# Attention in a fused kernel: the neighbour-key probabilities of two heads transposed as one 128x128 block, and one softmax multiplication in place of two

## The chip, the cores and the metric

The kernel runs on one core of one Trainium2 chip. The metric is the device time of one execution in microseconds (us). Lower is better.

## The reference

Sliding-window attention over 4 sequences of 576 tokens, 8 heads of 64 features, then a product of two projections with two more matrices behind it, then a feed-forward with SiLU. All outputs are float32; the weights come as float64.

```python
scores = np.matmul(q, k.transpose(0, 1, 3, 2)) / np.sqrt(64)
mask = (rel >= 0) & (rel < 64)              # rel = position of query - position of key
attn = softmax(where(mask, scores, -1e9))   # sum + 1e-9 in the denominator
x = (attn @ v) as [2304 tokens, 512]
x = ((x @ w1) * (x @ w2)) @ w3 @ w_out      # 512 -> 1024 -> 1024 -> 512
h = x @ w_in                                # 512 -> 2048
out = (h * sigmoid(h)) @ w_out2             # 2048 -> 512
```

## The kernel before

Activations lie transposed, features on partitions. A float32 operand of a product is split into two parts, hi and lo, of type float32r, and three products of parts are summed in PSUM.

The attention is cut into 72 groups: 18 units of 128 tokens times 4 pairs of heads. A token sees itself and the 63 tokens before it, so a unit needs its own 128 keys and the 64 before them: 192 columns of scores for each head. Those 64 earlier keys matter to the unit's first 64 tokens alone. A group passes through these steps, each with its line:

- `scores` (L242, L247): two products of 192 columns, one for each head, and from group 17 on a third product of 384 columns (L247) for the low part. Groups 0 to 16 are "plain": they multiply in float32 itself, with 64 rows of the array and without L247. VectorE then adds the mask and finds the maximum (L253).
- `exps` (L264): ScalarE's exponential, in place in the tile `sm`, with the row sums in `rs`.
- `normalise` (L272 to L278): VectorE makes the reciprocal of the sums and multiplies. It does so in two instructions: the first 64 tokens' columns of the earlier keys, both heads, go to a tile of their own, `sp` (64 partitions x 128), and the columns of the own keys stay in `sm` (128 partitions x 256).
- `transposes` (L286, L287): TensorE makes three transposes into the PSUM tile `t`: two of 128x128 from `sm`, one for each head, and one of `sp`, which has 64 partitions.
- `split_t` (L293 for plain groups; L297 to L302 for the others): ScalarE and VectorE copy `t` to SBUF as hi and lo parts `pt`. Only columns 0 to 319 of `t` are read.
- `values` (L312, L313 for plain groups; L319, L320 for the others): the product with v, into `o`; L323 to L327 add its four parts into `xr`.

The order is written out by hand. `half(h)` issues half a step of this pipeline: an even half issues the transposes of group g-1, the scores of group g, the copies of `t` and the exponentials; an odd half issues normalise of group g, values of group g-1 and what prepares later groups (L219, L223, L226, L79, L82). Each engine works through its instructions in the order in which they are issued.

The halves lie between other work. In `phase_w` (up to some 115.8 us of the profile) 28 halves go between the products of w3 with w_out (L452) and the conversion of weights from float64 (L106 to L134). In `phase_a`, called for each of six blocks of 384 tokens, one half goes ahead of each of 24 units, and a unit is 12 matmuls of 384 columns (L480, then L500). The attention's halves end with the fifth block; the sixth block has none, and the feed-forward (L602, L621) follows.

The masks come by three transfers from DRAM (L418, L424, L432), in one queue with the chunks of weights (L99). The host packs q, k and v so that each group's keys are one run of 384 columns.

Of the kernel before, what the change touches and what calls it, by code (L numbers as in the profile page):

```python
# [42 lines left out]
def tile_window_attention_ffn(ctx, tc, qkv, mask, ident, w1, w2, w3t, w_out, w_in, w_out2, out):  # L43
    """Sliding window attention, then p = (x w1)(x w2), x2 = p (w3 w_out), out = silu(x2 w_in) w_out2.

    Activations are kept transposed (features on partitions). Every float32 operand of a product
    is split exactly into hi + lo, two float32r parts, and hi*hi + hi*lo + lo*hi are summed in PSUM
    (the attention's second product takes all four; w3 w_out and the first groups of the attention
    are products in float32 itself).
    """  # L50
    nc = tc.nc
# [9 lines left out]

    mask_sb = att.tile([128, 3, 192], F32, name="mask_sb", tag="mask", bufs=1)
    id_sb = att.tile([128, 128], F32, name="id_sb", tag="ident", bufs=1)
# [4 lines left out]
    def slot(name, tag, dims, dtype=F32, pool=None, bufs=1):  # L68
        """A tile [128, *dims] in a slot of the tag's size (1024 words for a chunk of weights)."""
        t = (pool or main).tile([128, SLOTS.get(tag, 1024)], dtype, name=name, tag=tag, bufs=bufs)  # L70
        n = int(np.prod(dims))
        letters = "abcd"[: len(dims)]
        sizes = {x: d for x, d in zip(letters[1:], dims[1:])}
        return t[:, :n].rearrange(f"p ({' '.join(letters)}) -> p {' '.join(letters)}", **sizes)

    def split(hi, lo, src, eng_hi, eng_lo):
        """src (float32) = hi + lo, both float32r."""
        if eng_hi == "act":
            nc.scalar.copy(out=hi, in_=src)  # L79
        else:  # L80
            (nc.vector if eng_hi == "dve" else nc.gpsimd).tensor_copy(hi, src)
        (nc.vector if eng_lo == "dve" else nc.gpsimd).tensor_tensor(  # L82
            out=lo, in0=src, in1=f32(hi), op=ALU.subtract
        )

    PASSES = ((0, 0), (0, 1), (1, 0))

# [1 line left out]
    class Chunk:  # L89
        """A chunk of weights on its way: its words are in a slot of their own, and its parts take  # L90
        that slot over (`place`), or the float32 goes to `out`."""

# [16 lines left out]
        def stage1(self):  # L109
            """Round to the nearest float32: the high word less 896 exponents, three bits further left, its sign,  # L110
            and the low word's top three bits, rounded. In parts."""
            b = self.b

            def fraction():
                nc.vector.tensor_scalar(out=b, in0=b, scalar1=3, scalar2=None, op0=ALU.logical_shift_left)  # L115

            def sign():
                nc.vector.scalar_tensor_tensor(  # L118
                    out=b, in0=self.high, scalar=-0x80000000, in1=b, op0=ALU.bitwise_and, op1=ALU.bitwise_or
                )  # L120
                x = b if self.out is None else self.out.bitcast(I32)
                nc.gpsimd.tensor_tensor(out=x, in0=b, in1=self.r, op=ALU.add)  # L122

            return fraction, sign
# [25 lines left out]
    def fill(n=1):  # L150
        """Parts of stages that go between other instructions of VectorE that wait for one another."""
        for _ in range(min(n, len(parts))):
            parts.pop(0)()

    def steps_to(n, lo=(nc.vector,), keep=0):
        """Chunk t has its stages in steps t, t + 1, t + 3 and t + 4."""
        while done["step"] < min(n, len(line)):
# [18 lines left out]

# [1 line left out]
    NG = NU * NPAIR  # L178
    LAST_HALF = 2 * NG + 2
    qk_raw, v_raw, qk_st, v_st, s_st, p_st = {}, {}, {}, {}, {}, {}  # L180
    pt = {}
    sm = [att.tile([128, 2, 192], F32, name=f"sm{i}", tag=f"sm{i}", bufs=1) for i in range(2)]
    sp = [att.tile([64, 2, 64], F32, name=f"sp{i}", tag=f"sp{i}", bufs=1) for i in range(2)]
    k_lo = [att.tile([128, 384], F32R, name=f"klo{i}", tag=f"klo{i}", bufs=1) for i in range(2)]
# [5 lines left out]
    def plain(g):  # L190
        """The first groups multiply in float32 itself: more of TensorE's time, which the start has, and
        less of the other engines'."""
        return g < PLAIN
# [42 lines left out]
    def scores(g):  # L236
# [3 lines left out]
        for h in range(2):  # L240
            # The start also marks head 1's part as unwritten.
            nc.tensor.matmul(  # L242
# [8 lines left out]
        for h in range(2):  # L251
            # -(scores), and the least of them: minus the maximum.
            nc.vector.tensor_tensor_reduce(  # L253
                out=sm[g % 2][:, h, :], in0=s_ps[:, h, :], in1=mask_sb[:, mask_kind(place(g)[0]), :],
                op0=ALU.add, op1=ALU.min, scale=-(D ** -0.5), scalar=3.0e38, accum_out=nm[:, h : h + 1],
# [12 lines left out]
    def normalise(g):  # L268
        _, rs = s_st.pop(g)
        x, before = sm[g % 2], sp[g % 2]  # L270
        fill()
# [3 lines left out]
        fill()  # L275
        for dst, src in ((before, x[0:64, :, 0:64]), (x[:, :, 64:192], x[:, :, 64:192])):
            by = rs[0 : dst.shape[0]].unsqueeze(2).to_broadcast(list(dst.shape))
            nc.vector.tensor_tensor(out=dst, in0=src, in1=by, op=ALU.mult)  # L278

    def transposes(g):  # L280
        """The scores of the unit's own keys, by head; then those of the 64 keys before (which only the
        unit's first 64 tokens see) with head 0 on partitions 0-63 and head 1 on the others."""
        x = sm[g % 2]
        t_ps = psa.tile([128, 320], F32, name=f"t{g}", tag="t")
        for h in range(2):
            nc.tensor.transpose(t_ps[:, h * 128 : h * 128 + 128], x[:, h, 64:192], id_sb)  # L286
        nc.tensor.transpose(t_ps[:, 256:320], sp[g % 2].rearrange("p h n -> p (h n)"), id_sb[0:64, 0:64])  # L287
        return t_ps

    def split_t(g, t_ps):  # L290
        if plain(g):
            p_st[g] = p_w[g % 2]
            nc.scalar.copy(out=p_st[g], in_=t_ps)  # L293
            return
# [34 lines left out]
    def half(h):  # L329
        """Half a step of the attention's pipeline: group g is in its four stages in halves  # L330
        2g .. 2g + 3."""
        g, odd = divmod(h, 2)
# [8 lines left out]
        else:  # L341
# [7 lines left out]
            if g < NG:  # L349
                prep_v(g)  # L350
            # A slot is free again when its last group has been read.
            for x in range(g + 2, g + 5):
# [20 lines left out]

# [1 line left out]
    W_HALVES = 28  # L375
# [84 lines left out]

# [1 line left out]
    def phase_a(blk, hooks):  # L462
# [55 lines left out]
    with tc.manual_schedule():  # L518
# [7 lines left out]

# [1 line left out]
        end = ctx.enter_context(tc.tile_pool(name="end", bufs=1, side="right"))  # L528
# [10 lines left out]
        def x2_load(j, o=None):  # L539
            """The first block comes in four parts, between the weights."""  # L540
            n = x2t[j].shape[-1]
# [31 lines left out]
        def hooks5(n):  # L573
            if n == 0:
                nc.scalar.activation(out=sig, in_=sig, func=AF.Sigmoid)
            # Five chunks have slots at once, nine more from unit 8 on, eight from unit 16 on.
            loads_to(begin + (5 if n < 8 else 14 if n < 16 else 22))
# [73 lines left out]
def packed_qkv(q, k, v):  # L651
    """Per unit of 128 tokens and pair of heads, by partition: q (features, head 0, then head 1),
    q by head (features, twice), k by head of the
    192 tokens that end with the unit's last (features, twice), v of the unit's tokens by head,
    v of the 64 tokens before (head 0, then head 1)."""
    qt = q.transpose(3, 1, 0, 2).reshape(D, H, T)
# [5 lines left out]
    for u in range(NU):  # L662
        for c in range(NPAIR):
            hs = slice(2 * c, 2 * c + 2)
            for h, half in enumerate((slice(0, 64), slice(64, 128))):
                g[u, c, half, 0:128] = qt[:, 2 * c + h, u * 128 : (u + 1) * 128]
                g[u, c, half, 128:384] = qt[:, hs, u * 128 : (u + 1) * 128].reshape(D, 256)
                g[u, c, half, 384:768] = kt[:, hs, u * 128 + 64 : u * 128 + 256].reshape(D, 384)
            g[u, c, :, 768:896] = vt[u * 128 + 128 : u * 128 + 256, hs].reshape(128, 128)
# [3 lines left out]

def masks():
    r = np.arange(128)[:, None]
    c = np.arange(192)[None, :]
    band = (c >= r + 1) & (c <= r + WIN)
    first = band & (c >= 64)
    across = band & ((r < 64) | (c >= 128))
    m = np.where(np.stack([band, first, across], 1), 0.0, MASKED)  # L680
    return np.ascontiguousarray(m.astype(np.float32))

# [29 lines left out]
```

## Time and profile before

| | us |
|---|---|
| median of 3 runs (915.32 to 916.92) | 915.89 |
| span of the profiled execution | 914.5 |
| what the median has beyond the span | 1.4 |
| TensorE (PE) busy | 890.3 |
| VectorE (DVE) busy | 518.9 |
| ScalarE (ACT) busy | 492.3 |
| GpSimd (POOL) busy | 443.7 |

The span runs from the first to the last instruction of the profiled execution. Of that execution's own time the profile gives the span alone, so what lies around it is taken as the 1.4 us by which the median is longer. PE's matmuls overlap, so a busy PE says only that there was always a matmul under way. PEld is PE's loading of weights, which runs beside the matmuls.

### The profile page before, as it was taken

The numbers are of one execution on the slowest core, as the hardware profiler recorded it, in microseconds if no ns is written. First come the engines' busy times: TensorE is split into PE (matmuls) and PEld (weight loads), VectorE is DVE, ScalarE is ACT, GpSimd is POOL, SyncE is SP. The second block draws the span as 40 slices with busy tenths as digits, with TensorE's granted clock in tenths as the row PEclk, the third lists the DMA queues.
The fourth block names the chain that finished last, engine by engine and source line by source line (L and its number), as shares of the span: only waits on it lengthen the run. The fifth ranks groups of instructions, "written<-read, shape, count | busy, mean of one in ns | idle before, by whom it ended". The sixth has DMA issues, their size and how long they took to land.

```text
span 914.5 us, 13373 instructions
## 1 busy us (share of the span) xinstructions
PE 890.3 (97%) x4430; PEld 745.5 (82%) x4430; DVE 518.9 (57%) x1274; ACT 492.3 (54%) x1219; POOL 443.7 (49%) x470
## 2 busy tenths in 40 slices
PE   5999899999999999999999998999999999999998
PEld 2444379999999999999999876888888888888896
DVE  5989677877877877877578799311111111111111
ACT  6676567777777777777466677222222222222222
POOL 4669556556556455456288668422332232223222
PEclk9999899999999999999999999999999999999999
DMA  8976313332332332332377600110011000100100
GB/s 270 291 222 219 118 51 109 104 105 87 113 98 93 118 105 87 113 96 71 112 265 273 248 0 1 47 47 0 1 47 47 0 1 24 47 1 0 40 7 24
DMA packets 39396, 84.62 MB, mean 93 GB/s; under 512 B 4320, under 2 KB 17632, under 8 KB 39328
## 3 DMA queue, kind: packets, MB, share of 16 engines
q1 hardware_dynamic: 33280, 74.33, 24.8%
q10 hardware_dynamic: 6048, 9.44, 2.8%
q8 instruction: 35, 0.57, 0.2%
q14 instruction: 33, 0.27, 0.1%
HBM read 74.32 MB, written 9.44 MB: 92 GB/s over the span
## 4 chain that ended last, share of the span: by engine, by line
PE 81%; DVE 8%; POOL 3%; DMA 3%; ACT 2%; issue 2%; SPq 0%; POOLq 0%; DVEq 0%
PE ab L480 19%; PE o L621 19%; PE h L602 18%; PE x L500 11%; PE s L242 3%; PE accw L452 3%; DVE cv_b L115 3%; DVE cv_b L118 2%; PE t L286 2%; PE t L287 1%; PE o L319 1%; POOL cv_b L122 1%; PE s L247 1%; DVE hl L134 1%; DMA words<-in_w_in 1%
## 5 line engine op out<-in xcount | busy, mean ns | idle before, releaser
L621 PE MATMUL o<-hl,g 128*128 128x512 f32 x864 | 213.7, 394 | 3.7 <-POOL g L82 3.3
L602 PE MATMUL h<-x2t,hl 128*128 128x512 f32 (+1 forms) x960 | 214.0, 372 | 0.0
L82 POOL TENSOR_TENSOR g<-sg,g 128x512 fp32r<-128x512 f32 (+1 forms) x80 | 95.9, 1198 | 243.0 <-ACT g L79 228.5
L608 DVE TENSOR_TENSOR sg<-h,sg 128x512 f32<-128x512 f32 (+1 forms) x80 | 51.0, 637 | 280.8 <-ACT sg L607 280.8
L602 PEld LDWEIGHTS h<-x2t,hl 128*128 128x128 f32 x960 | 170.1, 189 | 34.1
L621 PEld LDWEIGHTS o<-hl,g 128*128 128x128 f32 x864 | 160.9, 188 | 41.5 <-POOL g L82 6.0
L607 ACT ACTIVATE sg<-h 128x512 f32<-128x512 f32 (+1 forms) x80 | 44.3, 553 | 188.5 <-PE h L602 188.5
L480 PE MATMUL ab<-xa,hl 128*128 128x384 f32 x576 | 117.3, 338 | 0.0
L480 PE MATMUL ab<-xb,hl 128*128 128x384 f32 x576 | 115.6, 335 | 0.0
L480 PEld LDWEIGHTS ab<-xb,hl 128*128 128x128 f32 x576 | 101.6, 188 | 0.0
L480 PEld LDWEIGHTS ab<-xa,hl 128*128 128x128 f32 x576 | 99.8, 188 | 0.9 <-issue 0.7
L327 POOL TENSOR_TENSOR xr<-ot 128x128 f32<-128x128 f32 x55 | 33.1, 602 | 129.3 <-DVE ot L326 125.6
L122 POOL TENSOR_TENSOR cv_b<-cv_b,cv_r 128x512 int32<-128x512 int32 x48 | 76.0, 1584 | 40.1 <-DVE cv_b L118 25.3
L79 ACT CAST g<-sg 128x512 fp32r<-128x512 f32 (+1 forms) x80 | 46.3, 579 | 72.1 <-DVE sg L608 72.1
L118 DVE SCALAR_TENSOR_TENSOR cv_b<-words,cv_b 128x512 int32<-128x512 int32 x72 | 84.0, 1166 | 2.0
L264 ACT ACTIVATE sm<-sm,nm 128x192 f32<-128x192 f32 x144 | 64.5, 449 | 17.8 <-DVE nm L253 16.6
L223 POOL TENSOR_TENSOR klo<-qk,qkhi 64x192 fp32r<-64x192 f32 x110 | 69.8, 635 | 7.1 <-ACT qkhi L219 2.9
L500 PE MATMUL x<-p,wp 128*128 128x384 f32 x360 | 69.7, 336 | 0.0
L500 PEld LDWEIGHTS x<-p,wp 128*128 128x128 f32 x360 | 62.3, 188 | 0.2
L115 DVE TENSOR_SCALAR cv_b<-cv_b 128x512 int32<-128x512 int32 x72 | 56.0, 778 | 10.8 <-ACT cv_b L106 10.8
L106 ACT ACTIVATE cv_b<-words 128x512 f32<-128x512 f32 x72 | 48.2, 669 | 18.4 <-POOL hl L134 7.3
L253 DVE CUSTOM_DVE_ANT_0 sm<-s,mask_sb 128x192 f32<-128x192 f32 x144 | 45.7, 354 | 20.8 <-PE s L247 15.5
(82 smaller groups left out, 1299.3 us busy)
## 6 DMA issues: line engine op xcount, KB each, us to landing
qk<-in_qkv SPq DMA_DIRECT2D x55, 384.0 KB, 3.0
words<-in_w_out SPq DMA_DIRECT2D x24, 512.0 KB, 8.1
words<-in_w3t SPq DMA_DIRECT2D x16, 512.0 KB, 6.3
words<-in_w SPq DMA_DIRECT2D x16, 512.0 KB, 5.9
words<-in_w_in SPq DMA_DIRECT2D x16, 512.0 KB, 7.0
v<-in_qkv SPq DMA_DIRECT2D x72, 96.0 KB, 2.6
x2d<-x2s ACTq DMA_DIRECT2D x24, 192.0 KB, 1.9
out_x<-osb ACTq DMA_DIRECT2D x18, 256.0 KB, 2.1
```

The lines of the kernel that those rows point to most:

```text
L82: (nc.vector if eng_lo == "dve" else nc.gpsimd).tensor_tensor(out=lo, in0=src, in1=f32(hi), op=ALU.subtract)
L106: nc.scalar.activation(out=f32(self.b), in_=f32(self.high), func=AF.Copy, scale=2.0**-112)
L115: nc.vector.tensor_scalar(out=b, in0=b, scalar1=3, scalar2=None, op0=ALU.logical_shift_left)
L118: nc.vector.scalar_tensor_tensor(out=b, in0=self.high, scalar=-0x80000000, in1=b, op0=ALU.bitwise_and, op1=ALU.bitwise_or)
L122: nc.gpsimd.tensor_tensor(out=x, in0=b, in1=self.r, op=ALU.add)
L223: nc.gpsimd.tensor_tensor(out=k_lo[g % 2][hs, h * 192 : h * 192 + 192], in0=t[hs, n], in1=f32(hi[hs, n]), op=ALU.subtract)
L264: nc.scalar.activation(out=x, in_=x, func=AF.Exp, scale=-1.0, bias=nm[:, h : h + 1], accum_out=rs[:, h : h + 1])
L480: nc.tensor.matmul(acc, lhsT=w[:, l, fs], rhs=x[k // 2][:, k % 2, r, :], start=(k == 0 and n == 0), stop=(k == 3 and n == 2),)
L500: nc.tensor.matmul(acc, lhsT=wp[f][:, l, o * 128 : (o + 1) * 128], rhs=p[f][:, r, :], start=(f == 0 and n == 0), stop=(f == 7 and n == 2),)
L602: nc.tensor.matmul(acc, lhsT=weights["in", f // 4, k][:, l, fs], rhs=x[:, k, r, :], start=(k == 0 and i == 0), stop=(k == 3 and i == 2),)
L608: nc.vector.tensor_tensor(out=sg, in0=acc, in1=sg, op=ALU.mult)
L621: nc.tensor.matmul(oacc[t], lhsT=g[:, l, t * 128 : (t + 1) * 128], rhs=weights["out", f][:, r, :], start=(f == 0 and i == 0), stop=(f == 1 ...
```

## The change

The two heads' probabilities for the 64 earlier keys are made to lie side by side in `sm`, and the third transpose takes that 128x128 block.

- The host packs the keys of head 0 as own, earlier, and those of head 1 as earlier, own. So the 384 columns of `sm` are: own keys of head 0, earlier keys of head 0, earlier keys of head 1, own keys of head 1. The mask has 256 columns (earlier, own, earlier again); head 0 takes columns 64 to 255, head 1 columns 0 to 191.
- `normalise` has one multiplication over 128x384, in place, instead of two, and `sp` is gone.
- The three transposes take columns 0, 256 and 128 of `sm`, 128 columns each, all with 128 partitions. `t` has 384 columns instead of 320; columns 320 to 383 are written and never read.

```diff
-    mask_sb = att.tile([128, 3, 192], F32, name="mask_sb", tag="mask", bufs=1)
+    mask_sb = att.tile([128, 3, 256], F32, name="mask_sb", tag="mask", bufs=1)
...
-    sp = [att.tile([64, 2, 64], F32, name=f"sp{i}", tag=f"sp{i}", bufs=1) for i in range(2)]
...
-                out=sm[g % 2][:, h, :], in0=s_ps[:, h, :], in1=mask_sb[:, mask_kind(place(g)[0]), :],
+                out=sm[g % 2][:, h, :], in0=s_ps[:, h, :], in1=mask_sb[:, mask_kind(place(g)[0]), 64 - 64 * h : 256 - 64 * h],
...
     def normalise(g):
-        x, before = sm[g % 2], sp[g % 2]
+        x = sm[g % 2]
...
-        for dst, src in ((before, x[0:64, :, 0:64]), (x[:, :, 64:192], x[:, :, 64:192])):
-            by = rs[0 : dst.shape[0]].unsqueeze(2).to_broadcast(list(dst.shape))
-            nc.vector.tensor_tensor(out=dst, in0=src, in1=by, op=ALU.mult)
+        nc.vector.tensor_tensor(out=x, in0=x, in1=rs.unsqueeze(2).to_broadcast([128, 2, 192]), op=ALU.mult)
 
     def transposes(g):
         x = sm[g % 2]
-        t_ps = psa.tile([128, 320], F32, name=f"t{g}", tag="t")
-        for h in range(2):
-            nc.tensor.transpose(t_ps[:, h * 128 : h * 128 + 128], x[:, h, 64:192], id_sb)
-        nc.tensor.transpose(t_ps[:, 256:320], sp[g % 2].rearrange("p h n -> p (h n)"), id_sb[0:64, 0:64])
+        t_ps = psa.tile([128, 384], F32, name=f"t{g}", tag="t")
+        x = x.rearrange("p h n -> p (h n)")
+        for i, at in enumerate((0, 256, 128)):
+            nc.tensor.transpose(t_ps[:, i * 128 : i * 128 + 128], x[:, at : at + 128], id_sb)
         return t_ps
...
-            nc.scalar.copy(out=p_st[g], in_=t_ps)
+            nc.scalar.copy(out=p_st[g], in_=t_ps[:, 0:320])
...
-                g[u, c, half, 384:768] = kt[:, hs, u * 128 + 64 : u * 128 + 256].reshape(D, 384)
+                own, before = kt[:, hs, u * 128 + 128 : u * 128 + 256], kt[:, hs, u * 128 + 64 : u * 128 + 128]
+                g[u, c, half, 384:768] = np.concatenate([own[:, 0], before[:, 0], before[:, 1], own[:, 1]], 1)
...
+    m = np.concatenate([m, m[:, :, 0:64]], 2)
```

On TensorE, between a unit of the x products (L500) and a unit of the ab products (L480), the order before is this (a row names the line, the operation, what is written and read, and the output's shape; x2 is two such instructions):

```order
L500 MATMUL x_3_3_4580<-q_3733,wp_954 128x384 x3
L286 MATMUL t_4658<-id_sb,sm_73 128x128 x2
L287 MATMUL t_4658<-id_sb,sp_75 128x64
L242 MATMUL s_4662<-qkhi_4551 128x192 x2
L247 MATMUL s_4662<-klo_76,qkhi_4551 128x384
L480 MATMUL ab_0_4678<-xa_4409,hl 128x384 x6
```

In the changed kernel the same place reads as follows (L499 and L479 are the former L500 and L480):

```order
L499 MATMUL x_3_3_4517<-q_3681,wp_938 128x384 x3
L286 MATMUL t_4594<-id_sb,sm_73 128x128 x3
L242 MATMUL s_4598<-qkhi_4488 128x192 x2
L247 MATMUL s_4598<-klo_74,qkhi_4488 128x384
L479 MATMUL ab_0_4614<-xa_4348,hl 128x384 x6
```

The one instruction with the 64-partition operand is gone from between the 128x128 transposes and the scores; nothing else changes its place on TensorE.

On VectorE, among the ab units of a block, from the reciprocal of a group's sums to the splitting of a later group's q (L226), the order before is:

```order
L274 RECIPROCAL rs_3050<-rs_3050 128x2
L278 TENSOR_TENSOR sp_75<-sm_73,rs_3050 64x128
L278 TENSOR_TENSOR sm_73<-sm_73,rs_3050 128x2x128
L325 TENSOR_TENSOR ot_3084<-o_3080,ot_3084 64x256
L326 TENSOR_TENSOR ot_3084<-o_3080,ot_3084 64x256
L226 TENSOR_TENSOR qkhi_3090<-qk_2944,qkhi_3090 64x256
```

And in the changed kernel:

```order
L274 RECIPROCAL rs_3007<-rs_3007 128x2
L276 TENSOR_TENSOR sm_73<-sm_73,rs_3007 128x384
L324 TENSOR_TENSOR ot_3040<-o_3036,ot_3040 64x256
L325 TENSOR_TENSOR ot_3040<-o_3036,ot_3040 64x256
L226 TENSOR_TENSOR qkhi_3046<-qk_2902,qkhi_3046 64x256
```

One instruction stands where two stood, and the neighbours are the same. ScalarE and GpSimd keep their instructions and their order; in the DMA queue only the three mask transfers grow from 128x192 to 128x256 elements.

## Rows read from the trace of the kernel before

**Rows 1.** The page: span, busy time of each engine, PE and its granted clock in 40 slices.

```profile
span 914.5 us, 13373 instructions
PE 890.3 (97%) x4430; PEld 745.5 (82%) x4430; DVE 518.9 (57%) x1274; ACT 492.3 (54%) x1219; POOL 443.7 (49%) x470
PEclk9999899999999999999999999999999999999999
```

**Rows 2.** Busy us of each engine by stage (x instructions), granted clock, DMA share, GB/s.

```profile
92.00:115.80 23.80, 19.93 (x63) 9.72 (x62) 16.53 (x39) 12.86 (x30) 11.34 (x11) 0.86 0.33 109
147.00:447.00 300.00, 300.00 (x1776) 285.26 (x1775) 241.74 (x820) 225.80 (x676) 164.86 (x249) 1.00 0.30 97
```

**Rows 3.** Chain of waits, 188 to 194.6 us: start, length, what.

```profile
187.97 0.22 PE t L286 x2
188.19 0.20 PE t L287
188.39 0.40 PE s L242 x2
188.79 0.20 PE s L247
188.99 2.09 PE ab L480 x12
191.08 0.24 PE o L319 x2
191.32 0.12 PE o L320
191.44 2.11 PE ab L480 x12
193.55 0.22 PE t L286 x2
```

**Rows 4.** PE's waits over the whole span: us in total, times, longest.

```profile
PE t L286 <- ACT cv_r L107: 5.3, 2, 3.9
PE t L286 <- DVE sm L278: 1.9, 3, 0.9
```

**Rows 5.** Timeline of PE from 56.4 us, a plain group: start, length, instruction.

```profile
56.47 0.38 PE L286 MATMUL t<-id_sb,sm 128*128 128x128 f32 x2
56.78 0.27 PE L287 MATMUL t<-id_sb,sp 64*128 64x64 f32 x1
56.89 0.87 PE L242 MATMUL s<-qk 64*128 64x192 f32 x4
57.69 1.98 PE L452 MATMUL accw<-wo,q 128*128 128x512 f32 x4
```

**Rows 6.** Groups by line and shape: busy us, mean ns, idle before and until what.

```profile
L287 PEld LDWEIGHTS t<-id_sb,sp 64*128 64x128 f32 x72 | 9.8, 136 | 12.1 <-issue 12.1
L278 DVE TENSOR_TENSOR sm<-sm,rs 128x256 f32<-128x256 f32 x72 | 29.4, 409 | 0.0
L278 DVE TENSOR_TENSOR sp<-sm,rs 64x128 f32<-64x128 f32 x72 | 22.0, 305 | 2.5
```

**Rows 7.** Timeline of several engines from 264.6 us, a group among ab units.

```profile
265.79 0.38 PE L286 MATMUL t<-id_sb,sm 128*128 128x128 f32 x2
...
268.20 0.45 DVE L302 TENSOR_TENSOR pt<-t,pt 64x64 fp32r<-64x64 f32 x2
...
269.13 0.28 PE L320 MATMUL o<-pt,vhl 128*128 128x256 f32 x1
...
269.54 0.28 DVE L278 TENSOR_TENSOR sp<-sm,rs 64x128 f32<-64x128 f32 x1
...
269.75 0.41 DVE L278 TENSOR_TENSOR sm<-sm,rs 128x256 f32<-128x256 f32 x1
...
271.20 0.14 PEld L286 LDWEIGHTS t<-id_sb,sm 128*128 128x128 f32 x1
```

**Rows 8.** DMA queue and a mask's transfer, 0 to 30 us.

```profile
q1 hardware_dynamic: 3417, 8.53, 89.0%
mask_sb<-in_mask SPq DMA_DIRECT2D x3, 96.0 KB, 5.8
```

**Rows 9.** Timeline from 245.6 us, a group among x units.

```profile
245.67 0.60 POOL L82 TENSOR_TENSOR vhl<-v,vhl 128x192 fp32r<-128x192 f32 x1
...
246.62 0.40 PE L319 MATMUL o<-pt,vhl 128*128 128x256 f32 x2
```

**Rows 10.** Timeline at 151 us, the group whose values waited longest.

```profile
150.88 0.61 POOL L82 TENSOR_TENSOR vhl<-v,vhl 128x192 fp32r<-128x192 f32 x1
...
151.60 0.47 PE L319 MATMUL o<-pt,vhl 128*128 128x256 f32 x2
```

## The prediction

> **What bounds the kernel now.** I read the page first. PE is busy for 890.3 of 914.5 us and its granted clock is at nine tenths in every slice [rows 1]. That is an average over stages, so I went to the stages next. From 147 to 447 us, where some 54 of the 72 groups of attention lie among the units with L480 and L500, PE is busy for all of 300.00 us at clock 1.00, that is at the upper level of 2.4 GHz. DVE has 241.74 us of work there and ACT 225.80 [rows 2]. A busy PE alone does not prove that its work is dense, since matmuls overlap. The chain of waits does: from one group's first transpose (187.97) to the next one's (193.55) every piece of the chain is PE's own [rows 3]. A group's period there is 5.58 us: transposes 0.22 + 0.20, scores 0.40 + 0.20, twelve matmuls 2.09, values 0.24 + 0.12, twelve matmuls 2.11. So in this stage whatever PE's queue loses or gains per group, the kernel loses or gains.
>
> PE's waits say the same from the other side. The transposes waited for the DVE multiplication, the place where the removed instruction stands, three times in the whole span, for 1.9 us in all [rows 4]. So the softmax multiplication is not what to look at. The transposes' own time is.
>
> Look at the chain's pieces [rows 3]. Two transposes of 128x128 take 0.22, so 0.11 each. The third has half the rows and half the columns and takes 0.20. The two score products behind it have 192 columns each and take 0.40, so 0.20 each, while values, with 256 columns, take 0.12 each. Small instructions are dear on both sides of the one with 64 rows (its tile reads 64*128, all the others 128*128). The plain groups show whether it is the transpose or the change of rows. There the scores have 64 rows too (64*128). From the small transpose at 56.78 to the scores at 56.89 is 0.11, and from the second big one to the small one is again 0.20 (0.31 from 56.47, less 0.11) [rows 5]. So going from 64 to 64 rows is cheap, and going from 128 to 64 is dear. PEld shows the cause: the weights of L287 come after an idle time of 12.1 us over 72 times, 0.17 each, in which it waited for nothing that the profile shows [rows 6]. Weights that are elsewhere loaded while the matmul ahead still runs are not loaded ahead here.
>
> **The change part by part.**
>
> *Third transpose, 128x128 instead of 64 rows.* It becomes like its two neighbours: 0.11 for 0.20, a saving of 0.09 [rows 3].
>
> *Scores behind it, groups 17 to 71.* With no 64-row tile ahead their weights can be loaded early. No row shows these products in that position. The nearest rows are the values: 0.12 with 256 columns, and the transposes: 0.11 [rows 3]. I take 0.23 for the two in place of 0.40, a saving of 0.17. The bounds are 0 (if the 0.20 were the scores' own) and 0.20 (if the product of L247, 0.20 as well, also came down by 0.03 to the 0.17 of an ab matmul, 2.09 / 12).
>
> Together 0.26 per group; the bounds are 0.09 and 0.29. Over 55 groups that makes 14.3 us, from 5.0 to 16.0. The last transposes, of group 71, have no scores behind them; with the first matmul behind them I count 0.2. That is 14.5.
>
> *Plain groups, 17 of them.* The change of rows moves: it is now between the third transpose and the scores, and no longer between the second and the third. Before: 0.11 + 0.20 + 0.11 up to the scores [rows 5]. After: 0.11 + 0.11 + 0.20, the same. I count 0.
>
> *DVE.* The two multiplications start 0.21 apart and the second takes 0.41 [rows 7], so 0.62 together. From 64x128 to 128x256 a multiplication grows from 0.28 to 0.41, so 0.13 per 128 elements [rows 7], and one of 384 should take 0.54. DVE gains 0.08 per group. In the phase with L480 and L500 that is hidden: the multiplication ends at 270.16 and the transposes' weights start at 271.20, 1.04 later [rows 7]. If that cover were gone, 0.08 for each of 55 groups, 4.4 us, would be gained. In the first 116 us, where PE once waits 3.9 us with DVE full ahead of it [rows 4], 14 groups times 0.08 is 1.1 at most; I take 0.2.
>
> *Masks.* Each of three transfers grows from 96 to 128 KB. Their queue is 89% busy in the first 30 us and moves 8.53 MB there [rows 8], so 0.28 MB per us; 32 KB is 0.11 us. The first (L418) is issued ahead of most weights. Between 0 and 0.34; I take 0.2, which cancels the item before.
>
> *What comes closer.* The saved time shortens the period, not the work of DVE, ACT and POOL. So the values come 0.26 nearer to the copies of `t` that they need. Among ab units the last copy (L302) ends at 268.65 and the product that reads it starts at 269.13 [rows 7], 0.48 between. Among x units POOL's low part of v ends at 246.27 and the values start at 246.62 [rows 9], 0.35 between. In the group that did wait, the matmul started 0.11 after the same POOL instruction had ended (151.49 to 151.60) [rows 10], so 0.11 is the least. After the change 0.48 becomes 0.22, still free; 0.35 becomes 0.09, which is just short. Four groups of twelve lie among x units, some 18 in all; at 0.03 each that costs 0.5. If all durations there spread as in the waiting group it would be a few us; this is the second rival.
>
> Sum: 914.5 - 14.5 + 0.5 = 900.5 for the span. With the 1.4 us by which the median is longer, 901.9, rounded to **902**. All that follows the fifth block is issued behind PE's work or waits for slots which that work frees, so I let it move as a whole.
>
> **The rivals.**
>
> *Half of it.* Only the third transpose gets cheaper, and the scores keep 0.40, because going from a float32 transpose to a float32r product costs that by itself. In rows of before this step never occurs without the change of rows, so nothing excludes it. The reverse step, from an ab matmul to a transpose, costs nothing (12 ab matmuls take 2.11 with a transpose next, 2.09 with values next) [rows 3]. It gives 915.9 - 5.0 = 911. The Trainium skill (TensorEngine Tiling (Array Packing), Tiling Modes, Key Properties) says that a change of the tiling mode drains the engine, and names no such cost for a change of type. By that rule this rival falls. Chance 0.10.
>
> *The other engines become the bound.* DVE has 241.74 of 300 us [rows 2]. Over some 54 groups that is 4.48 of 5.58 for each, and 4.40 of 5.32 afterwards. The engines work in order and pass each other results, ACT to DVE to POOL to PE, so a loop of waits can be longer than any one engine's sum. If half of the 14.3 us goes to new waits of the values for L302 or for POOL, the time is 909; if a third, 907. For it: the 0.35 of rows 9. Against it: 0.48 in the other two thirds of the groups. Chance 0.14.
>
> *Slower: the wide block is only more work.* Suppose that the dear steps stay: the 0.20 behind the second transpose belongs to the third place in `t` and the 0.40 to the scores. Then the third transpose streams 128 columns instead of 64. Two transposes of 128 columns start 0.11 apart, so 64 columns more are 0.055, and 56 groups give 3.1 us: 919. It decides from the point at which less than 0.055 of the 0.26 is saved. Against it stand the plain groups, in which the same transpose is followed at 0.11 [rows 5]. The Trainium skill (TensorEngine Tiling (Array Packing), Theoretical Speedup) speaks for it: it promises up to twice the rate to products whose contracted dimension is 64 or less, on smaller tiles, and this change gives a smaller tile up. The same section rests that on several tiles working at once. In this trace the neighbours on both sides have 128 rows, so nothing runs beside the small one. Chance 0.06.
>
> *No change.* Savings on PE come back as waits in full, in the weights' conversion from 447 to 575 us or elsewhere: 916. Nothing in the rows speaks for it but DVE's load. Chance 0.03.
>
> **How the numbers follow.** The forecast as worked out has 0.67. Its own range is 899.5 (0.29 per group, no new waits) to 905 (0.20 per group). The half has 0.10, the other engines 0.14, slower 0.06, no change 0.03. The range for 8 in 10 takes the forecast and the other engines' case: 898.5 to 909.5. That leaves out the half, the slower one and no change, 0.19. The measurement of this kernel can tell about 0.2% from no change, some 1.8 us. Faster by more than that: 0.67 + 0.10 + 0.14 = 0.91; within: 0.03; slower: 0.06.
>
> **What would show it.** In the chain of waits of a group among ab units: three transposes in some 0.33 instead of 0.42, the two scores in 0.23 to 0.25 instead of 0.40, a period of 5.32 instead of 5.58. PEld has no idle time ahead of the third transpose. The plain groups keep their length, with the dear step now ahead of the scores. The waits of the values for POOL and DVE, now next to nothing, may show up to 1 us in total. The end of the attention, at 447 us before, comes at some 433, and what follows keeps its length.
>
> It is wrong if the scores behind the transposes still take 0.40 (the half), or if PE waits for `pt` or `vhl` in most groups (the other engines). A third way is the clock: in the stage from 92 to 115.8 us it is 0.86 [rows 2], behind PE's longest wait for work of DVE and ACT. A shift of that wait could lengthen or shorten the stretch at the lower level, 1.2 GHz, by some us, with no part in the change's own reason.

## The result, and the profile after

The changed kernel takes 905.16 us (median of 4 runs, 904.8 to 906.0), the kernel before 916.18 in the runs beside it: a ratio of 0.9881, 95% interval 0.9867 to 0.9895. The profiled execution has a span of 903.0 us, 11.5 less than before [rows 1].

The page after, span and busy time:

```profile
span 903.0 us, 13301 instructions
PE 877.2 (97%) x4430; PEld 741.9 (82%) x4430; DVE 517.6 (57%) x1202; ACT 492.0 (54%) x1219; POOL 437.4 (48%) x470
```

PE is as busy by share as before. So the page does not show what was gained; the chain does. The chain of waits after, one group among ab units (start, length, what; a piece runs from the end of the record ahead to its own end), to be held against [rows 3]:

```profile
214.00 0.33 PE t L286 x3
214.33 0.20 PE s L242 x2
214.53 0.20 PE s L247
214.73 2.08 PE ab L479 x12
216.81 0.23 PE o L318 x2
217.05 0.19 PE o L319
```

Transposes and scores take 0.73 where they took 1.02: the third transpose costs 0.11, the two scores 0.20 together. Taken apart by the ends of their records (means of 55 groups), the first score falls from 0.29 to 0.10 and the second only from 0.12 to 0.11. So behind the 64-row transpose it was the first matmul that was dear. But values take 0.42 where they took 0.36. That is the part of the gain that was given back. Over the 54 groups 18 to 71, from the first transpose to the next unit's first matmul, the sum of the starts' distances falls from 55.0 to 39.6 us (0.285 per group, 0.29 in all but the first of them). Group 17, the first with such scores, gains nothing. Over the 55 groups of values the sum rises from 19.8 to 24.2.

A block of twelve groups, from its first ab matmul to the next block's, took 66.84 before and takes 64.35 after (mean of blocks 1 to 3), so the mean period of a group is 5.36 in place of 5.57. In these blocks it is 5.27 to 5.37 among ab units and 5.41 to 5.49 around x units.

The rest of the 11.5: the attention among the units gives 11.2. The first stage is 0.5 longer (its end goes from 115.8 to 116.3); in runs 2 and 5 below, which make the same transposes, it ends at 115.8, so this is not shown to be the change's doing. Behind the attention 0.8 is gained, and that is not shown to be its doing either. In both executions PE waits 2.21 us for GpSimd's part of `g` in the feed-forward, at 571.5 before and at 560.9 after. Before, ten matmuls behind it took 3.52, and the granted clock of the stretch from 560 to 580 us is 0.91, so a part of it ran at the lower level; after, the ten take 2.56 and the clock there is 1.00. Behind the same wait the ten take 4.07 in run 5 and 2.55 in run 2, and both have the change's transposes. The timeline after:

```profile
560.92 2.56 PE L620 MATMUL o<-hl,g 128*128 128x512 f32 x10 [2.21 <-POOL g L82]
```

The row of the kernel before, the same view:

```profile
571.50 3.52 PE L621 MATMUL o<-hl,g 128*128 128x512 f32 x10 [2.21 <-POOL g L82]
```

Where the values lose time is read from the timeline. First the kernel after among ab units, one full turn of ScalarE and VectorE, with the values:

```profile
200.95 0.48 ACT L485 COPY a<-ab 128x384 f32<-128x384 f32 x1
201.45 0.37 ACT L322 COPY ot<-o 64x256 f32<-64x256 f32 x1
201.83 0.36 ACT L323 COPY ot<-o 64x256 f32<-64x256 f32 x1
202.28 0.42 DVE L324 TENSOR_TENSOR ot<-o,ot 64x256 f32<-64x256 f32 x1
202.71 0.43 DVE L325 TENSOR_TENSOR ot<-o,ot 64x256 f32<-64x256 f32 x1
203.08 0.42 DVE L226 TENSOR_TENSOR qkhi<-qk,qkhi 64x256 fp32r<-64x256 f32 x1
203.54 0.56 DVE L487 TENSOR_TENSOR a<-ab,a 128x384 f32<-128x384 f32 x1
204.13 0.51 ACT L79 CAST p<-a 128x384 fp32r<-128x384 f32 x1 [0.83 <-DVE a L487]
204.55 0.36 ACT L296 CAST pt<-t 128x256 fp32r<-128x256 f32 x1
204.81 0.43 ACT L298 CAST pt<-t 64x64 fp32r<-64x64 f32 x2
205.27 0.46 ACT L264 ACTIVATE sm<-sm,nm 128x192 f32<-128x192 f32 x1
...
205.62 0.45 DVE L301 TENSOR_TENSOR pt<-t,pt 64x64 fp32r<-64x64 f32 x2
...
206.22 0.35 PE L319 MATMUL o<-pt,vhl 128*128 128x256 f32 x1
206.28 0.48 ACT L485 COPY a<-ab 128x384 f32<-128x384 f32 x1
```

Read it from the top: each piece starts within a tenth of a us of the end of the one above it. ScalarE copies an ab sum, then the values of the group before; VectorE adds them, splits q and multiplies; ScalarE copies p and only then `t`; then come the exponentials (the second, left out here, and the reading of its sum last until 206.26), and the next copy of an ab sum. One turn is 206.28 - 200.95 = 5.33. The last subtraction (L301) ends at 206.07 and the third values product (L319), which reads what it wrote, starts 0.15 later, which is as close as this pair comes in any group. Before, the distance was 0.48 [rows 7].

The kernel before has the same turn with room in it. There ScalarE waits for PE ahead of its copy of the ab sum:

```profile
269.09 0.48 ACT L486 COPY a<-ab 128x384 f32<-128x384 f32 x1 [0.25 <-PE ab L480]
```

Among ab units the turns before are 5.56 to 5.58 long, with a wait of 0.25 to 0.27 for PE in each. Without it 5.31 are left. After, the turns are 5.33 and that wait is gone.

Second, a group among x units, to be held against [rows 9]:

```profile
248.24 0.60 POOL L82 TENSOR_TENSOR vhl<-v,vhl 128x192 fp32r<-128x192 f32 x1
...
248.90 0.49 PE L318 MATMUL o<-pt,vhl 128*128 128x256 f32 x2
```

GpSimd's part of v ends at 248.84 and the values start 0.06 later, where it was 0.35; the two and the third product then take 0.52 instead of 0.36 in that group. In 14 of the 55 groups this distance is now 0.05 to 0.07. None of this shows as idle time of PE, since the matmul ahead is still under way in the record; it shows as longer distances between starts.

### The profile page after: what moved, and what is told of

Same layout as the page of the kernel before. It is cut to its first block, busy times and chain, and to the rows that moved or that the text cites. A ratio compares the mean times of both kernels' runs of the same rounds, so it can differ in the third digit from the quotient of the medians.

```text
span 903.0 us, 13301 instructions
## 1 busy us (share of the span) xinstructions
PE 877.2 (97%) x4430; PEld 741.9 (82%) x4430; DVE 517.6 (57%) x1202; ACT 492.0 (54%) x1219; POOL 437.4 (48%) x470
## 4 chain that ended last, share of the span: by engine, by line
PE 78%; DVE 9%; POOL 4%; DMA 4%; issue 3%; ACT 2%; SPq 1%; POOLq 0%; DVEq 0%; ACTq 0%
PE o L620 18%; PE h L601 18%; PE ab L479 18%; PE x L499 10%; DVE cv_b L115 3%; PE accw L451 3%; PE t L286 2%; DVE cv_b L118 2%; PE s L242 2%; PE o L318 2%; DVE hl L134 1%; POOL cv_b L122 1%; PE s L247 1%; DMA qk<-in_qkv 1%; PE o L319 1%
## 5 line engine op out<-in xcount | busy, mean ns | idle before, releaser
L479 PE MATMUL ab<-xa,hl 128*128 128x384 f32 x576 | 116.6, 337 | 0.0
L479 PE MATMUL ab<-xb,hl 128*128 128x384 f32 x576 | 115.6, 335 | 0.0
L479 PEld LDWEIGHTS ab<-xb,hl 128*128 128x128 f32 x576 | 101.4, 188 | 0.0
L479 PEld LDWEIGHTS ab<-xa,hl 128*128 128x128 f32 x576 | 99.4, 188 | 0.9 <-issue 0.7
L122 POOL TENSOR_TENSOR cv_b<-cv_b,cv_r 128x512 int32<-128x512 int32 x48 | 74.0, 1542 | 43.5 <-DVE cv_b L118 35.3
L326 POOL TENSOR_TENSOR xr<-ot 128x128 f32<-128x128 f32 x55 | 33.1, 602 | 118.3 <-DVE ot L325 116.3
L118 DVE SCALAR_TENSOR_TENSOR cv_b<-words,cv_b 128x512 int32<-128x512 int32 x72 | 77.4, 1076 | 2.0
L115 DVE TENSOR_SCALAR cv_b<-cv_b 128x512 int32<-128x512 int32 x72 | 64.5, 896 | 10.0 <-ACT cv_b L106 10.0
L499 PE MATMUL x<-p,wp 128*128 128x384 f32 x360 | 69.6, 335 | 0.0
L499 PEld LDWEIGHTS x<-p,wp 128*128 128x128 f32 x360 | 62.2, 188 | 0.1
```

The source lines that it names most:

```text
L118: nc.vector.scalar_tensor_tensor(out=b, in0=self.high, scalar=-0x80000000, in1=b, op0=ALU.bitwise_and, op1=ALU.bitwise_or)
L479: nc.tensor.matmul(acc, lhsT=w[:, l, fs], rhs=x[k // 2][:, k % 2, r, :], start=(k == 0 and n == 0), stop=(k == 3 and n == 2),)
L499: nc.tensor.matmul(acc, lhsT=wp[f][:, l, o * 128 : (o + 1) * 128], rhs=p[f][:, r, :], start=(f == 0 and n == 0), stop=(f == 7 and n == 2),)
```

## The experiments

Each run was timed beside the kernel before, whose median lay between 916.1 and 917.0.

**1. The single multiplication alone.** The key layout and the multiplication of the change, but the third transpose from 64 partitions:

```diff
-        for i, at in enumerate((0, 256, 128)):
+        for i, at in enumerate((0, 256)):
             nc.tensor.transpose(t_ps[:, i * 128 : i * 128 + 128], x[:, at : at + 128], id_sb)
+        nc.tensor.transpose(t_ps[:, 256:320], x[0:64, 128:256], id_sb[0:64, 0:64])
```

> New key layout and the single multiplication over 128x384, but the third transpose takes only the first 64 partitions again (64 rows, as before). Theory (the gain is TensorE's change of rows, and the multiplication is hidden): the time of the kernel before, 916 +- 1, with the third transpose and the two scores at 0.20 + 0.40 per group again. Rival (fewer and shorter VectorE instructions carry the gain): 905 to 908. A mixture would lie between, with 4.4 us (0.08 for 55 groups) as the most that VectorE can give: 911.5.

Measured: 916.29 us, ratio to before 1.0003 (0.9992 to 1.0014). Its chain of waits has the old pieces back:

```profile
215.51 0.22 PE t L286 x2
215.73 0.20 PE t L287
215.93 0.40 PE s L242 x2
216.33 0.20 PE s L247
```

So the single multiplication is worth nothing that can be measured while PE still needs 5.57 per group, and the scores behind the transposes are dear again when the 64-row transpose stands ahead of them.

**2. The wide transpose alone.** The change with two multiplications in place:

```diff
-        nc.vector.tensor_tensor(out=x, in0=x, in1=rs.unsqueeze(2).to_broadcast([128, 2, 192]), op=ALU.mult)
+        early, flat = x.rearrange("p h n -> p (h n)")[0:64, 128:256], x.rearrange("p h n -> p (h n)")
+        early = early.rearrange("p (h n) -> p h n", h=2)
+        own = flat.rearrange("p (b n) -> p b n", b=3)[:, 0:3:2, :]
+        for part in (early, own):
+            by = rs[0 : part.shape[0]].unsqueeze(2).to_broadcast(list(part.shape))
+            nc.vector.tensor_tensor(out=part, in0=part, in1=by, op=ALU.mult)
```

> The changed kernel, but with two multiplications in place (64x128 for the earlier keys, 128x256 for the own keys) ahead of the three 128x128 transposes. Theory (TensorE's change of rows): 905, within 1 us of the changed kernel, since VectorE's 0.08 per group ends about 1 us ahead of the transposes. Rival (VectorE carries the gain): 912 to 916. If VectorE's queue is now part of the loop that the values wait for, 0.08 for up to 55 groups, at most 909.5.

Measured: 905.58 us, ratio 0.9885 (0.9867 to 0.9904). So the gain is TensorE's. A block takes 64.49 in its profile, 0.14 more than in the changed kernel; if the single multiplication adds anything to the wide transpose, it is this, some 0.7 us over five blocks, which the timed runs don't tell from nothing.

**3. VectorE's first subtraction earlier.**

```diff
         nc.scalar.copy(out=b[:, :, 0, :], in_=own)
+        nc.vector.tensor_tensor(out=b[:, :, 1, :], in0=own, in1=f32(b[:, :, 0, :]), op=ALU.subtract)
         for h, hs in HEADS:
             nc.scalar.copy(out=a[hs, h, 0], in_=before[hs])
-        nc.vector.tensor_tensor(out=b[:, :, 1, :], in0=own, in1=f32(b[:, :, 0, :]), op=ALU.subtract)
```

> The changed kernel, with VectorE's first subtraction of the copies of t (the own keys' low part) issued right after ScalarE's first copy instead of after all three. In the changed kernel the second values product starts 0.148 us after VectorE's last subtraction in some 25 groups, which is as close as it comes. Theory (the values wait for VectorE's last subtraction, which is late because the first one waits for ScalarE's third copy): the last subtraction ends some 0.3 earlier, the values in groups among ab units return from 0.40-0.44 to 0.36, 36 groups times 0.06 are 2 us: 903. Rival (the values wait for GpSimd's part of v everywhere, or ScalarE's queue itself is the bound): 905, no change.

Measured: 935.04 us, ratio 1.0199 (1.0182 to 1.0217). That is 30 us slower than the changed kernel, far from both expectations. (What the expectation calls the second values product is the third, L319.) Its waits between 147 and 430 us (who waits for whom, us in total, times, longest):

```profile
ACT pt L299 <- DVE pt L297: 32.7, 47, 1.3
...
DVE pt L301 <- ACT pt L299: 23.4, 47, 0.5
```

ScalarE's second and third copy of `t` now wait for VectorE's first subtraction, which reads the same PSUM tile, and VectorE's others wait for them. The copy that waits writes another SBUF tile than that subtraction, so the PSUM tile is all that the two share: in this program the two engines' reads of one PSUM tile take turns. With all of ScalarE's reads first there is one handing over; with the edit there are three. The run doesn't tell whether the values wait for L301, but it shows that a longer turn of ScalarE and VectorE goes into the time.

**4. The split of v ahead of the split of q and k.**

```diff
+            early = PLAIN + 2 <= g < NG
+            if early:
+                prep_v(g)
             for x in (g + 1, g + 2):
                 if x - g == (1 if plain(x - 2) else 2):
                     prep_qk(x)
-            if g < NG:
+            if g < NG and not early:
                 prep_v(g)
```

> The changed kernel, with the split of v (ScalarE's and GpSimd's parts) issued ahead of the split of q and k from group 19 on. In the changed kernel the first values product starts 0.055 us after GpSimd's low part of v in some 19 groups, those at and around the x units, and there the values take 0.46 to 0.53 instead of 0.36. Theory (these groups wait for GpSimd): the low part of v comes 1.2 earlier, and 19 groups times 0.10 to 0.15 are 2 to 3 us: 902.5. Rival (behind that wait stands the one for VectorE's last subtraction, 0.16 ahead in the same groups, and ScalarE's split of q and k now comes 0.35 later): 904 to 906.

Measured: 927.48 us, ratio 1.0117 (1.0098 to 1.0135), 22 us slower than the changed kernel; both expectations missed. Here the chain of waits leaves PE altogether and shows the loop by itself:

```profile
212.99 0.56 DVE a L490
...
214.00 0.37 ACT pt L296
...
214.72 0.99 ACT sm L264 x4
215.71 0.02 issue
215.73 0.34 ACT a L488
...
216.60 0.38 ACT ot L323
216.98 0.01 issue
216.99 0.35 ACT vhl L79
217.34 0.75 ACT qkhi L219
218.09 0.02 issue
218.12 0.62 DVE qkhi L226
218.74 0.03 issue
218.77 0.56 DVE a L490
```

One turn is 218.77 - 212.99 = 5.78, and the split of v (0.35) is now a part of it. In the changed kernel it stood behind the split of q and k (L219), outside.

**5. The copy of p out of the loop.** The split of p is issued after the next unit's half of the attention:

```diff
         def unit(n):
             halves_to(W_HALVES + 24 * blk + n + 1)
+            while later:
+                f = later.pop(0)
+                split(p[f][:, 0], p[f][:, 1], a_of[f][:, 1], "act", "pool")
             hooks(n)
...
-                split(p[f][:, 0], p[f][:, 1], a_sb[:, 1], "act", "pool")
+                a_of[f] = a_sb
+                later.append(f)
```

> The changed kernel, with the split of each product p (ScalarE's copy and GpSimd's subtraction behind VectorE's L487) issued after the next unit's half of the attention instead of ahead of it. Theory (a loop of waits from the values over VectorE's additions, L226 and L487, to ScalarE's copy of p and from there to the copies of t and back to the values is now as long as the period): the copies of t no longer stand behind the copy of p, the values among ab units return from 0.40-0.44 to 0.36, some 36 groups times 0.06 are 2 us: 903. Rival (the values are late because of VectorE's or ScalarE's whole load, not because of that link): 905, or more, since work is only shifted.

Measured: 903.69 us, ratio 0.9865 (0.9851 to 0.9878). Its chain of waits among ab units:

```profile
213.35 0.33 PE t L286 x3
213.68 0.20 PE s L242 x2
213.88 0.20 PE s L247
...
216.17 0.23 PE o L318 x2
216.40 0.12 PE o L319
...
218.62 0.33 PE t L286 x3
```

The third values product is back at 0.12 and the period at 218.62 - 213.35 = 5.27. In 37 of 55 groups the values take 0.36 again (6 in the changed kernel), and a block takes 64.01 instead of 64.35; the sum of the values' distances falls from 24.2 to 22.1. The intervals of this ratio and of the changed kernel's overlap a little, so the link is shown by the rows of the trace, and its price of some 1.5 us less surely.

**6. The split of v ahead of the values' copies.**

```diff
+            first = PLAIN + 2 <= g < NG
+            if first:
+                prep_v(g)
             if 1 <= g <= NG:
                 values(g - 1)
...
-            if g < NG:
+            if g < NG and not first:
                 prep_v(g)
```

> The changed kernel, with the split of v issued ahead of the values' own copies from group 19 on, so that ScalarE does it while it would wait for the values, and not between those copies and the split of q and k as in the run that moved v by half as far. Theory (around x units the values wait for GpSimd's low part of v, and the run before lost its 22 us only because it put ScalarE's 0.35 into the loop of waits): 19 groups gain 0.10 to 0.15, 2 to 3 us: 902.5, or 903.5 if the wait for VectorE's last subtraction stands close behind. Rival (any earlier split of v delays the copies that the additions wait for): 906 or more.

Measured: 915.16 us, ratio 0.9978 (0.9967 to 0.9989): a miss; the rival (906 or more) holds. I had taken ScalarE to be waiting for the values there; in the turn shown above it goes from L485 to L322 without a gap, so the split of v lies in the loop here too. A block takes 66.43.

**7. Both moves, 5 and 6.** The edits are those two together.

> Both moves of the two runs beside it. Theory (the 4.4 us by which the values grew are two waits, one for VectorE's last subtraction among ab units and one for GpSimd's part of v around x units): both go, 901 +- 1, and a period of 5.29 in all groups. Rival (one wait only hides the other, or ScalarE's and VectorE's load is the bound): 903 to 905.

Measured: 904.22 us, ratio 0.9869 (0.9856 to 0.9883). With the loop cut, the move that cost 10 us by itself costs nothing. But it brings nothing either: a block takes 63.84, 0.17 less than in run 5, but in its profile the first stage ends at 116.9, 1.0 later; and around x units the values still take up to 0.56. There GpSimd's part of v is now long done, and they wait for L301. They start 0.15 behind it, as close as that pair comes. So two waits lay close together there, as the expectation's rival says.

**8. As 7, with 64 rows ahead of plain scores.**

```diff
+        if plain(g + 1):
+            nc.tensor.transpose(t_ps[:, 256:320], x[0:64, 128:256], id_sb[0:64, 0:64])
+        else:
+            nc.tensor.transpose(t_ps[:, 256:384], x[:, 128:256], id_sb)
```

> As the run beside it with both moves, and the third transpose takes 64 rows again where plain scores, which have 64 rows, follow it (groups 0 to 15). In the changed kernel a plain group's transposes and scores take 0.046 longer than before (the first score matmul 0.267 to the next in place of 0.219, less 0.003). Theory (TensorE sets the first stage too): 16 groups times 0.046 are 0.7 us less than the run beside it. Rival (there the conversion of weights sets the time): no difference beyond 0.3 us.

Measured: 902.86 us, ratio 0.9851 (0.9838 to 0.9865). The difference of 1.4 us to run 7 is twice what was expected, and its runs reach from 901.98 to 905.75. Runs 10 and 11 ask again.

**9. The copy of p later, in the kernel before.** The edit of run 5.

> The kernel before (64-row transpose, two multiplications), with the split of p issued after the next unit's half of the attention, as in the run that did so to the changed kernel. Theory (the loop of ScalarE and VectorE is some 5.33 us long in both kernels and was hidden under TensorE's 5.57 before the change): no gain, 916 to 917, a period of 5.57. Rival (the order with the split of p later is better by itself, in the conversion stages too): 914.5 to 915.5, as it gave 1.5 us to the changed kernel.

Measured: 916.33 us, ratio 1.0001 (0.9992 to 1.0011), and a block takes 66.84 as before. The same link that costs the changed kernel some 1.5 us costs the kernel before nothing, where ScalarE has 0.25 to 0.27 to spare in each turn. The loop was there and hidden; the change uncovered it.

**10. The changed kernel with 64 rows ahead of plain scores, and nothing else.** The edit of run 8.

> The changed kernel, with the third transpose at 64 rows where plain scores, which have 64 rows, follow it (groups 0 to 15), and nothing else. Per plain group TensorE saves 0.046. Theory (TensorE sets the first stage): 0.7 us less than the changed kernel, 904.5 against 905.2. Rival (conversion of weights sets that stage): 905.2 +- 0.3. The first stage differs by about 1 us between profiled executions, so a difference below 0.5 decides nothing.

Measured: 905.03 us, ratio 0.9878 (0.9862 to 0.9894). Against 905.16 that is no difference that these runs can tell.

**11. Runs 5 and 10 together.**

> The changed kernel with the split of p later and with 64 rows for the third transpose ahead of plain scores. Theory: 903.7 of the run with the split of p alone, less 0.7: 903. Rival (no gain in the first stage): 903.7. It is also the smallest set of edits that may beat both kernels.

Measured: 902.95 us, ratio 0.9859 (0.9841 to 0.9878). It is 0.7 below run 5, with intervals that overlap. In its profiled execution and in that of run 10 the first stage ends at 116.5, not earlier than the changed kernel's 116.3. In all the traces this end lies between 115.7 and 118.6. So whether the plain groups' 0.046 is worth anything stays open. Runs 5, 8 and 11 are the fastest here, 902.9 to 903.7, and cannot be told apart; all of them have the copy of p later.

## Why the prediction was right, and where it was off

The forecast was 902, its range 898.5 to 909.5; 905.16 was measured. The direction and the cause hold, a term of the sum was mis-sized. The time lies well inside the stated range and just above the forecast's own, which ends at 905, and it came by another sum: 0.285 in place of 0.26 per group, and 4.4 us in place of 0.5 given back.

- *TensorE is the bound, and the row change is the cost.* Right. Undoing it alone gives back everything (run 1), doing it alone gives everything (run 2).
- *Third transpose 0.20 to 0.11.* Right: three take 0.33.
- *Scores 0.40 to 0.23.* Right in kind: 0.20. But "0.20 each" was the mean of two unlike ones: by the ends of the records the first took 0.29 and the second 0.12, and almost all of the saving is the first one's. With the product of L247 unchanged at 0.20, the sum per group is 0.285 where 0.26 was forecast, close to its upper bound of 0.29. The half rival is out: the step from a float32 transpose to a float32r product costs nothing by itself (their starts lie 0.03 apart after). The Trainium skill's sentence that a change of the tiling mode drains the engine (TensorEngine Tiling (Array Packing), Tiling Modes, Key Properties) fits these rows and names no price; here it is 0.29 per group for one 64-row transpose among 128-row work. The slow rival is out with it.
- *Plain groups 0.* Right in kind, slightly off in size. The rows of a plain group after, with PE's loading of weights for the plain scores below them:

```profile
56.37 0.49 PE L286 MATMUL t<-id_sb,sm 128*128 128x128 f32 x3
56.79 0.91 PE L242 MATMUL s<-qk 64*128 64x192 f32 x4
L242 PEld LDWEIGHTS s<-qk 64*128 64x128 f32 x68 | 11.6, 202 | 10.1 <-DMA qk<-in_qkv 7.3 <-issue 2.8
```

  With 0.11 from transpose to transpose the third starts at 56.59, and the scores 0.20 later. So the dear step has moved, as forecast, to where the rows now change. The idle time of PEld that no wait explains has moved with it: it was 0.17 ahead of each 64-row transpose [rows 6], and now 2.8 us stand ahead of the plain scores, some 0.17 for each of 16 groups, where there were none. This is the strongest sign that the change of rows is the cost, and not the small transpose. A plain group is 0.046 longer from the first transpose to its last score; the 0.046 is the first score's. The first stage was 0.5 longer in the profile; runs 2, 5, 10 and 11 don't show that the one causes the other.
- *DVE.* Right that it is hidden. The multiplication takes 0.57 (mean of 72) where 0.54 was expected, so 0.05 is saved and not 0.08; run 1 shows that it brings nothing by itself, and run 2 that the gain does not need it:

```profile
L276 DVE TENSOR_TENSOR sm<-sm,rs 128x384 f32<-128x384 f32 x72 | 40.9, 568 | 2.5
```

- *What comes closer, 0.5.* This is the term that was mis-sized: the values gave back 4.4 us (24.2 less 19.8). Around x units I had the right wait and too small a price: 0.35 became 0.06 (so the 0.11 that I took for the least was not the least), and all three products together lose 0.1 to 0.2 per group there instead of 0.03. Among ab units I had it free: 0.48 less 0.26 is 0.22, and at least 0.15 is needed. That step treated the copies of `t` as tied to PE alone, so that the distance would shrink by what PE saves and by no more. They are tied to ScalarE's and VectorE's own turn of 5.33, which is longer than the 5.27 to 5.29 that PE needs (run 5). Where PE would be faster than that turn, the distance shrinks from group to group until PE waits.
- *The other engines become the bound.* This rival, to which I gave 0.14, came true in part: among ab units the period settles at some 5.33 instead of the 5.27 to 5.29 of run 5. By the prediction's own sign it came true in most groups, since the values take longer than 0.36 in 49 of 55; but they gave back 4.4 of 15.4 us and not half. It had the loop in words and no length for it. The trace of the kernel before holds one: 5.58 less ScalarE's wait of 0.25 to 0.27 for PE is 5.31.
- *The clock.* As a third way I named the lower level in the stage from 92 us on. It had no part: the granted clock there is 0.86 before and after. My reading of the page was loose, though: the row of slices shows 8 and not 9 in the slice of that stage [rows 1].

What adds up: 54 groups times 0.285 are 15.4, and 0.3 for the last group's transposes, which have no scores behind them (0.2 was forecast); less 4.4 for the values and 0.3 for the units leaves 11.0. The stage itself shows 11.2; the difference lies in the units ahead of 142 us, which the sum leaves out. The first stage takes 0.5, and 0.8 is gained behind the attention, where the ten matmuls alone make up 0.96.

## What to carry to other kernels

- One instruction on fewer rows among full-array matmuls is paid for twice, on the way in (0.09 here) and on the way out (0.19), and the second time in the first matmul behind it. Look for the distance between starts, not for the small instruction's own duration. Padding it to the full array can be cheaper; here by 11 us.
- Before a saving on the bounding engine is booked, add up the longest loop of waits among the others over one period. The saving ends there, however low their busy share is. Here, from 147 to 436.5 us after, VectorE is busy for 239.0 of 289.5 us (83%) and ScalarE for 226.1 (78%), and their loop still filled the period (busy us by engine, PE, PEld, DVE, ACT, POOL):

```profile
147.00:436.50 289.50, 289.05 (x1778) 283.24 (x1778) 239.03 (x767) 226.09 (x677) 165.20 (x249) 1.00 0.32 101
```

- A move in the order that is free in one kernel (run 9) is worth something once the bound has come closer (run 5), and one that looks free because an engine "waits there" must be checked in the timeline: run 6 lost 10 us.

## What the hardware showed that was not expected

- The scores' 0.40 was not theirs. The two with 192 columns take 0.20 together behind a 128-row transpose and 0.40 behind a 64-row one, and the difference is in the first of them (0.29 against 0.10).
- A late operand costs more than one matmul: where the values start 0.06 behind the part of v, the three products together take 0.52 instead of 0.36, with no idle time in PE's record. That the weights' loading, which comes late there too, is the reason was argued from the rows and not tried.
- One and the same wait of 2.21 us was followed by ten matmuls in part at the lower clock in one execution (3.52) and at the upper in another (2.56).
